# The end of the first batch: when w_out's last pieces are converted, batch 1's x is turned and half of the second products run

## The chip, the core and the metric

The kernel runs on one core of a Trainium2 chip. The core's engines run side by side, each through its own instructions in a fixed order, and wait for one another through semaphores: TensorE (PE, with its weight loads shown as PEld), VectorE (DVE), ScalarE (ACT), GpSimd (POOL, all but unused here), and SyncE (SP), which here only issues DMAs. The metric is the time of one execution on the device, in microseconds (us); smaller is better.

## The reference, cut to what matters

Eight batches of 512 tokens and 32 states, in 8 heads of 64, go through a cross attention in both directions. Its rows, 544 per batch and 512 wide, then go through two dense layers with an activation between them.

```python
# x: (8, 8, 512, 64)   state: (8, 8, 32, 64)   w_in: (512, 2048)   w_out: (2048, 512)
scores = scale * np.matmul(x, state.transpose(0, 1, 3, 2))
a = np.exp(scores - scores.max(-1, keepdims=True)); a /= a.sum(-1, keepdims=True) + 1e-09
xread = np.matmul(a, state)
scores2 = scale * np.matmul(state, x.transpose(0, 1, 3, 2))
a2 = np.exp(scores2 - scores2.max(-1, keepdims=True)); a2 /= a2.sum(-1, keepdims=True) + 1e-09
sread = np.matmul(a2, x)
x = np.concatenate([xread, sread], axis=2)      # then (B*544, 512)
h = x @ w_in
g = h * erf(np.maximum(h, 0.0) + np.log1p(np.exp(-np.abs(h))))    # h * erf(softplus(h))
out = g @ w_out
```

The two weight matrices arrive as 64-bit floats and are turned into 32-bit floats on the chip.

## The kernel before

**Weights.** `weight` fetches a piece of 1 MB into a buffer `raw` (three of them in turn) and converts it there: two ACT operations (L127, L128) and three DVE operations (L129, L130, L131). w_in and w_out come in eight pieces each, two pieces of each for one group of hidden features. There are four groups (`NG`) of four tiles of 128 features.

**The first batch.** Batch 0 is worked while the weights arrive, group by group, in the loop at L600. `mixed(0, g)` multiplies the states into w_in (L328: small products, 64 rows deep and 32 columns wide each, in two PSUM banks named `at`), and ACT and DVE copy one bank each to `m` (L330). `hidden` forms four banks `h` of first products (L420) in two PSUM buffers; from each, ACT writes a softplus (L427) and DVE a copy `hs` (L428), and both must be done before the buffer takes the next bank but one. `finish` takes erf on ACT (L432) and multiplies on DVE (L433). `project` is the second product (L438): 16 matmuls for a group, four for each of the banks `o` 0 to 3. It runs one group late: the second product of group 2 is issued behind the first product of group 3.

**The last group, g = 3.** Here other work is woven in. `rest` is the second half of batch 0's attention: turn the weights (L210 on PE, copies L212 on ACT), read the tokens (L224), scale (L229 on DVE), turn the result (L234). `states(1)` (L162) and `attention(1)` begin batch 1: x is turned on DVE (L284), PE forms the scores (L177, again 64 by 32 tiles), ACT copies them to `sc` (L181), and a chain on DVE and ACT makes the attention weights `aT` (L293 to L302). `prepare(1, ...)` makes `m` for two groups of batch 1 by four more calls of `mixed`, with `combine_m` adding them up on DVE (L339 to L342). `combine_a` does the same for `aT` (L352 to L355). `combine_w` (L460) makes sums of w_out's blocks, three of them into the `raw` buffers; all later second products use them.

In the kernel before, the two last pieces of w_out are fetched with the others, but their conversion is put off: `convert` (L625) holds the functions, and L637 issues them behind the copies of batch 1's scores (`marks[0]`).

**From batch 1 on** the first products (L375, `hidden7`) and the second products (L488, `project7`) use seven products where eight would stand, and the second product of the group before is interleaved with the first product of the group that runs. The first time, while batch 1's first group runs, the group that is interleaved is group 3 of batch 0 (L438, `pending` at L650), and its four banks are copied out at L447.

**What sets the order.** The program is written as a stream of calls, and a scheduler places each engine's instructions. `tc.issue_after(m)` (in `behind`) holds what stands within it until the instruction `m` in the scheduler's order. A group of instructions once placed runs in that order on its engine, whatever becomes ready first.

In the names, `o_336` to `o_339` are the four banks of batch 0's second products, and `o_1011` to `o_1014` those of batch 1's first half.

Of the kernel before, what the change touches and what calls it, by code (L numbers as in the profile page):

```python
# [8 lines left out]
F32 = mybir.dt.float32  # L9
U32 = mybir.dt.uint32  # L10
ALU = mybir.AluOpType
# [5 lines left out]
def kernel(  # L17
# [17 lines left out]
    nc = tc.nc  # L35
# [70 lines left out]

    fetched = []

    def weight(dst, src, shape, later):

        if src.dtype == F32:
            fetched.append(nc.sync.dma_start(out=dst, in_=src))
            return lambda: None
        i = shape[1]
        raw = act.tile([P, 2 * shape[0] * i], U32, name="raw", bufs=3)
        fetched.append(nc.sync.dma_start(out=raw.rearrange("p (o i) -> p o i", i=2 * i),
                                         in_=src.bitcast(U32)))  # L120
        words = raw.rearrange("p (n w) -> p n w", w=2)
        lo, hi = words[:, :, 0], words[:, :, 1]
        dst = dst.rearrange("p o i -> p (o i)")
        d = dst.bitcast(U32)

        def convert():
            nc.scalar.activation(out=dst, in_=hi.bitcast(F32), func=ACTF.Copy, scale=2.0 ** -112)  # L127
            nc.scalar.activation(out=lo, in_=lo, func=ACTF.Copy, scale=2.0 ** -29)  # L128
            nc.vector.tensor_scalar(d, d, 3, None, op0=ALU.logical_shift_left)  # L129
            nc.vector.tensor_tensor(d, d, lo, op=ALU.add)  # L130
            return nc.vector.scalar_tensor_tensor(out=d, in0=hi, scalar=0x80000000, in1=d,  # L131
                                                  op0=ALU.bitwise_and, op1=ALU.bitwise_or)
        return convert if later else convert()

    gw = GF * P

    def weights_in(j):
        return weight(w_in[:, j],
                      moe_w_in[:, 2 * P * j:2 * P * j + 2 * P].rearrange("(k p) f -> p k f", p=P),
                      (NK, 2 * P), False)  # L140

    def weights_out(j, later=False):
        return weight(w_out[:, 2 * j:2 * j + 2, :],
                      moe_w_out[2 * P * j:2 * P * j + 2 * P].rearrange("(t p) e -> p t e", p=P),
                      (2, d_model), later)

    spare = ps_o.tile([P, d_model], F32, name="o3")

# [21 lines left out]
    def scores(b, xT):  # L170


        s2 = [ps_at.tile([P, S], F32, name="at") for _ in range(2)]
        for i in range(NI):
            for e in range(2):
                r, q = slice(D * e, D * e + D), slice(Ns * i, Ns * i + Ns)
                on_pe = nc.tensor.matmul(out=s2[e][q, :], lhsT=stT[b][r, q], rhs=xT[r, i, :],  # L177
                                         start=True, stop=True)
        sc = att.tile([P, 2, S], F32, name="sc")
        for e in range(2):  # L180
            last = nc.scalar.copy(sc[:, e], s2[e])  # L181
        marks[:] = last, on_pe
        return sc, last
# [94 lines left out]
    def attention(b):  # L278

        xq = xq_t.pop(b)
        xT = att.tile([P, NI, S], F32, name="xT")
        nc.vector.transpose(out=xT.rearrange("p i t -> p (i t)"),  # L284
                            in_=xq.rearrange("p i m d -> p (i m d)"))
        if b + 1 < B:
            load_xq(b + 1)
        sc, _ = scores(b, xT)
        yield
        both = att.tile([P, NI, S], F32, name="xT")  # L290
        aT[b] = keep.tile([P, 2, S], F32, name="aT")
        for e in range(2):
            nc.vector.transpose(out=both[:, e], in_=sc[:, e])  # L293
            a = both[:, e].rearrange("p (k n) -> p k n", n=Ns)
            m1 = small.tile([P, NC * NI], F32, name="m1")
            nc.vector.reduce_max(out=m1, in_=a, axis=AX.X)
            nc.vector.tensor_tensor(a, a, over(m1), op=ALU.subtract)  # L297
            nc.scalar.activation(out=a, in_=a, func=ACTF.Exp, scale=scale)
        z2 = weigh_tokens(sc, both[:, 2:4])
        for e in range(2):  # L300
            normalise(both[:, e].rearrange("p (k n) -> p k n", n=Ns))
            nc.vector.transpose(out=aT[b][:, e], in_=both[:, e])  # L302
        yield
        a2T = turn_weights(both[:, 2:4])
        yield
        sn = read_tokens(b, a2T, z2)
        if b + 1 < B:
            load_x(b + 1)
        yield
        turn_read(b, sn)  # L310
        yield

    m_t = {}

    def mixed(b, g, parts=1):

        m_t[b, g] = mix.tile([P, 2, gw], F32, name="m")
        return [mixed_part(b, g, j, parts) for j in range(parts)]

    def mixed_part(b, g, j, parts):  # L320
        n = gw // parts
        mg = m_t[b, g][:, :, n * j:n * j + n]
        fs = slice(2 * g + j, 2 * g + j + 2 // parts)
        ps = [ps_at.tile([P, gw], F32, name="at")[:, 0:n] for _ in range(2)]
        for i in range(NI):
            for e in range(2):
                r, q = slice(D * e, D * e + D), slice(Ns * i, Ns * i + Ns)
                nc.tensor.matmul(out=ps[e][q, :], lhsT=stT[b][r, q],  # L328
                                 rhs=w_in[r, fs, i, :], start=True, stop=True)
        return nc.scalar.copy(mg[:, 0], ps[0]), nc.vector.tensor_copy(mg[:, 1], ps[1])  # L330

    def combine_m(b, g):

# [97 lines left out]
    def finish(s, hs):  # L431
        return (nc.scalar.activation(out=s, in_=s, func=ACTF.Erf),  # L432
                nc.vector.tensor_tensor(s, s, hs, op=ALU.mult))  # L433

    def project(gT, g, acc, rs=range(NC), ts=range(GF)):
        for r in rs:
            for i in ts:
                nc.tensor.matmul(out=acc[r], lhsT=gT[:, i, P * r:P * r + P],  # L438
                                 rhs=w_out[:, GF * g + i, :],
                                 start=(g == 0 and i == 0),  # L440
                                 stop=(g == NG - 1 and i == GF - 1))
                yield
# [90 lines left out]
    def begins(b):  # L533
        return 1 - b % 2
# [24 lines left out]
    def done(steps):  # L559
        for _ in steps:  # L560
            pass
# [4 lines left out]
                side[n]()  # L566
            yield

    def prepare(b, g):
        for j in range(2):  # L570
            mixed(b, 2 * g + j)
        combine_m(b, g)

    def begin(on_pe, on_act, on_dve):
# [5 lines left out]
    def behind(marks, f, *args):  # L580
        with ExitStack() as order:
            for m in marks:
                order.enter_context(tc.issue_after(m.ins))
            return f(*args)
# [15 lines left out]
    for g in range(1, NG):  # L600

        if g == 1:
            for j in range(2):
                made = behind(at, weights_in, 2 + j)
            done(project(gT, 0, acc, range(2)))
            at, = mixed(0, 1)
            behind([made], weights_out, 2)
            made = behind(at, weights_out, 3)
            done(project(gT, 0, acc, range(2, 3)))
        else:  # L610
            if g == 2:
                behind([made], weights_in, 4)
                behind(banks[1][:2], weights_in, 5)
                done(project(gT_, 0, acc, range(3, 4), range(GF - 1)))
            else:
                for j in range(2):
                    behind(banks[j][:2], weights_in, 2 * g + j)
            at, = mixed(0, g)
            if g == 2:
                done(project(gT_, 0, acc, range(3, 4), range(GF - 1, GF)))  # L620
            if g < NG - 1:
                for j in range(2):
                    behind(at, weights_out, 2 * g + j)
        if g == NG - 1:
            convert = [weights_out(2 * g + j, True) for j in range(2)]  # L625
            behind(fetched[-1:], load_st)
            behind(fetched[-1:], load_xq, 1)
            behind(done_, rest)
            load_x(1)
            states(1)  # L630
            turn = attention(1)
        gT_, (gT, hs, banks) = gT, hidden(0, range(GF * g, GF * g + GF), 0, S)
        at = done_ = finish(gT, hs)
        if g == NG - 1:

            behind([banks[1][1], at[0]], next, turn)
            for f in convert:  # L637
                behind(marks[:1], f)
            done(behind(marks[1:], project, gT_, g - 1, acc, range(1)))
            next(turn)  # L640
            prepare(1, begins(1))
            at = [combine_a(1)]
            done(behind(marks[1:], project, gT_, g - 1, acc, range(1, NC)))
        elif g > 1:
            done(project(gT_, g - 1, acc))
    prepare(1, 1 - begins(1))
    done(turn)
    last = behind(at, combine_w)

# [67 lines left out]
```

## Time and profile before

| | before |
|---|---|
| median of 3 runs | 783.2 us (782.07 to 783.7) |
| the profiled execution | 784.38 us, of which its span is 782.6 us |
| PE busy | 760.7 us, 97% of the span |
| DVE busy | 504.4 us, 64% |
| ACT busy | 383.6 us, 49% |
| chain of work that ended last | PE 79%, DVE 9%, ACT 4% |

A row of the timeline gives the start in us, the length in us, engine, line, operation, tiles (written and read), shape and count, and in brackets the idle time before it with what ended it. The length of a merged row reaches to the end of its last instruction, which overlaps the next row; the step from one row's start to the next is what it costs the engine. A 32-bit matmul leaves two records, so "x8" of L438 is four matmuls (a transpose by the identity, L210, leaves one). A row of the window view gives the stretch, its length, the busy time of PE, PEld, DVE, ACT and POOL with the number of records, the granted TensorE clock (1.00 is full speed), the DMA share and GB/s. In the view of waits a row reads: who waited, for whom, total us, how often, the longest.

### The profile page before, as it was taken

The numbers are of one execution on the slowest core, as the hardware profiler recorded it, in microseconds if no ns is written. First come the engines' busy times: TensorE is split into PE (matmuls) and PEld (weight loads), VectorE is DVE, ScalarE is ACT, GpSimd is POOL, SyncE is SP. The second block draws the span as 40 slices with busy tenths as digits, with TensorE's granted clock in tenths as the row PEclk, the third lists the DMA queues.
The fourth block names the chain that finished last, engine by engine and source line by source line (L and its number), as shares of the span: only waits on it lengthen the run. The fifth ranks groups of instructions, "written<-read, shape, count | busy, mean of one in ns | idle before, by whom it ended". The sixth has DMA issues, their size and how long they took to land.

```text
span 782.6 us, 11868 instructions
## 1 busy us (share of the span) xinstructions
PE 760.7 (97%) x4980; PEld 600.8 (77%) x4980; DVE 504.4 (64%) x757; ACT 383.6 (49%) x490; POOL 0.7 (0%) x6
## 2 busy tenths in 40 slices
PE   8998989989999999999999999999999999999997
PEld 7533431679888888888888888888889889998886
DVE  3888558786768666675767576947595665453431
ACT  5867543375446444554455444554464444443320
POOL 0000000000000000000000000000000000000000
PEclk9999995999999999999999999999999999999999
DMA  7675830332004200302012200320000000000001
GB/s 219 214 240 192 180 59 14 82 68 55 28 1 82 54 14 14 66 27 45 28 30 53 54 28 2 80 56 28 1 28 1 28 1 28 1 28 1 28 0 28
DMA packets 106557, 42.71 MB, mean 55 GB/s; under 512 B 96008, under 2 KB 96008, under 8 KB 106504
## 3 DMA queue, kind: packets, MB, share of 16 engines
q1 hardware_dynamic: 104392, 41.43, 19.9%
q8 instruction: 39, 0.64, 0.3%
q10 hardware_dynamic: 2112, 0.52, 0.3%
q14 instruction: 14, 0.11, 0.0%
HBM read 33.03 MB, written 8.91 MB: 54 GB/s over the span
## 4 chain that ended last, share of the span: by engine, by line
PE 79%; DVE 9%; ACT 4%; issue 1%; DVEq 0%; ACTq 0%
PE o L488 40%; PE h L375 20%; PE h L420 6%; PE o L438 6%; PE at L328 5%; ACT s L432 2%; DVE s L433 1%; DVE hs L382 1%; PE at L224 1%; ACT L432 1%; DVE ot L498 1%; PE at L210 1%; DVE m L197 1%; DVE z L187 1%; DVE xT L297 1%
## 5 line engine op out<-in xcount | busy, mean ns | idle before, releaser
L433 DVE TENSOR_TENSOR s<-s,hs 128x2048 f32<-128x2048 f32 x34 | 77.9, 2292 | 76.2 <-ACT s L432 76.1
L488 PE MATMUL o<-w_out,s 128*128 128x256 f32 x480 | 118.2, 381 | 0.0
L488 PE MATMUL o<-raw,hs 128*128 128x256 f32 x480 | 116.4, 385 | 0.0
L488 PE MATMUL o<-w_out,hs 128*128 128x256 f32 x480 | 115.4, 381 | 0.0
L488 PEld LDWEIGHTS o<-raw,hs 128*128 128x128 f32 x480 | 88.4, 190 | 31.3 <-issue 20.1
L381 ACT ACTIVATE s<-hs 128x512 f32<-128x512 f32 x112 | 70.6, 630 | 71.8 <-DVE hs L382 71.5
L488 PEld LDWEIGHTS o<-w_out,hs 128*128 128x128 f32 x480 | 90.0, 190 | 16.3 <-issue 4.2
L375 PEld LDWEIGHTS h<-aT,m 128*128 128x128 f32 x672 | 86.3, 195 | 11.6 <-issue 5.2
L488 PEld LDWEIGHTS o<-w_out,s 128*128 128x128 f32 x480 | 85.6, 192 | 8.4
L375 PE MATMUL h<-aT,m 128*128 128x128 f32 x672 | 88.1, 280 | 2.4 <-ACT s L385 2.4
L382 DVE TENSOR_TENSOR hs<-hs,h 128x512 f32<-128x512 f32 x84 | 57.5, 684 | 44.5 <-PE h L375 44.3
L438 PE MATMUL o<-w_out,s 128*128 128x512 f32 x128 | 63.6, 637 | 5.3 <-DVE w_out L131 4.4
L382 DVE TENSOR_TENSOR hs<-s,h 128x512 f32<-128x512 f32 x56 | 38.4, 686 | 46.8 <-PE h L375 46.4
L432 ACT ACTIVATE s<-s 128x2048 f32<-128x2048 f32 x34 | 65.0, 1911 | 0.4
L375 PE MATMUL h<-sy,sx 128*128 128x128 f32 x448 | 59.2, 275 | 0.0
L488 PE MATMUL o<-raw,s 128*128 128x256 f32 x240 | 57.7, 379 | 0.0
L375 PEld LDWEIGHTS h<-sy,sx 128*128 128x128 f32 x448 | 56.6, 192 | 1.5
L385 ACT COPY s<-h 128x512 f32<-128x512 f32 x28 | 16.3, 582 | 81.8 <-PE h L375 81.8
L438 PEld LDWEIGHTS o<-w_out,s 128*128 128x128 f32 x128 | 24.3, 200 | 37.8 <-issue 28.9
L390 ACT COPY hs<-h 128x512 f32<-128x512 f32 x28 | 16.3, 583 | 63.7 <-PE h L375 63.7
L488 PEld LDWEIGHTS o<-raw,s 128*128 128x128 f32 x240 | 43.6, 191 | 4.8
L328 PE MATMUL at<-w_in,stT 64*32 64x512 f32 (+1 forms) x528 | 43.8, 624 | 1.4 <-ACT sc L181 0.7
(100 smaller groups left out, 914.9 us busy)
## 6 DMA issues: line engine op xcount, KB each, us to landing
raw<-in_moe_w_in_dram SPq DMA_DIRECT2D x8, 1024.0 KB, 5.3
raw<-in_moe_w_out_dram SPq DMA_DIRECT2D x8, 1024.0 KB, 5.0
out_dram<-ot SPq DMA_DIRECT2D x32, 256.0 KB, 2.0
x<-in_x_dram SPq DMA_DIRECT2D x60, 128.0 KB, 2.9
xq<-in_x_dram SPq DMA_DIRECT2D x112, 64.0 KB, 2.1
x<-in_x_dram ACTq DMA_DIRECT2D x4, 128.0 KB, 3.9
out_dram<-ot SPq DMA_DIRECT2D x8, 64.0 KB, 1.7
st<-in_state_dram SPq DMA_DIRECT2D x8, 56.0 KB, 4.4
```

What stands on the lines that cost most here:

```text
L187: nc.vector.reduce_sum(out=z1, in_=a, axis=AX.X)
L328: nc.tensor.matmul(out=ps[e][q, :], lhsT=stT[b][r, q], rhs=w_in[r, fs, i, :], start=True, stop=True)
L375: last = nc.tensor.matmul(out=bank[:, q], lhsT=x[:, q], rhs=y, start=(first and i == 0), stop=(i == GF - 1), skip_group_check=not first)
L381: nc.scalar.activation(out=s[:, k], in_=hs[:, k], func=ACTF.Softplus)
L382: add = lambda o, x, y: nc.vector.tensor_tensor(o, x, y, op=ALU.add)
L385: nc.scalar.copy(m1, p)
L390: nc.scalar.copy(c11, p)
L420: on_pe = nc.tensor.matmul(out=hp[:, n * j:n * j + n], lhsT=lhsT, rhs=rhs, start=(k == 0), stop=(k == len(ops) - 1))
L432: return (nc.scalar.activation(out=s, in_=s, func=ACTF.Erf), nc.vector.tensor_tensor(s, s, hs, op=ALU.mult))
L433: nc.vector.tensor_tensor(s, s, hs, op=ALU.mult))
L438: nc.tensor.matmul(out=acc[r], lhsT=gT[:, i, P * r:P * r + P], rhs=w_out[:, GF * g + i, :], start=(g == 0 and i == 0), stop=(g == NG - 1 a ...
L488: nc.tensor.matmul(out=acc[bank][:, E2 * c:E2 * c + E2], lhsT=lhs[:, i, :], rhs=rhs[:, g, i, :], start=(first and i == 0 and c == 0), stop ...
```

## The change

Three things move, all around group 3 of batch 0; what is computed stays as it was.

- **w_out's two last pieces** are converted like the others, issued behind the copy `m` of `mixed(0, 3)`; `convert` and the argument `later` go.
- **batch 1's x is turned** (and its scores formed) behind the DVE copy of the last bank of group 3's first product, and `finish` of group 3 is held behind that turn. `finish` stood ahead of it.
- **half of group 2's second product** (banks 2 and 3) is issued behind the scores; before, that was three banks of four, with one bank ahead of the `prepare`. Now banks 0 and 1 are written ahead of it.
- The four `mixed` calls of the two `prepare` calls at this place have both their copies on ACT; before, one was on ACT and one on DVE.

```diff
@@ weight
-        def convert():
-            nc.scalar.activation(out=dst, in_=hi.bitcast(F32), func=ACTF.Copy, scale=2.0 ** -112)
...
-        return convert if later else convert()
+        nc.scalar.activation(out=dst, in_=hi.bitcast(F32), func=ACTF.Copy, scale=2.0 ** -112)
...
@@ attention
-        nc.vector.transpose(out=xT.rearrange("p i t -> p (i t)"),
+        turned = nc.vector.transpose(out=xT.rearrange("p i t -> p (i t)"),
...
         sc, _ = scores(b, xT)
+        marks.append(turned)
@@ mixed_part
-        return nc.scalar.copy(mg[:, 0], ps[0]), nc.vector.tensor_copy(mg[:, 1], ps[1])
+        return nc.scalar.copy(mg[:, 0], ps[0]), copy(mg[:, 1], ps[1])
@@ the loop over groups
-            if g < NG - 1:
-                for j in range(2):
-                    behind(at, weights_out, 2 * g + j)
+            for j in range(2):
+                behind(at, weights_out, 2 * g + j)
         if g == NG - 1:
-            convert = [weights_out(2 * g + j, True) for j in range(2)]
...
-        at = done_ = finish(gT, hs)
-        if g == NG - 1:
+        if g < NG - 1:
+            at = done_ = finish(gT, hs)
+        else:
 
-            behind([banks[1][1], at[0]], next, turn)
-            for f in convert:
-                behind(marks[:1], f)
-            done(behind(marks[1:], project, gT_, g - 1, acc, range(1)))
+            behind(banks[3][1:2], next, turn)
+            scored, turned = marks[1:]
+            behind([turned], finish, gT, hs)
+            done(project(gT_, g - 1, acc, range(2)))
             next(turn)
-            prepare(1, begins(1))
+            prepare(1, begins(1), nc.scalar.copy)
             at = [combine_a(1)]
-            done(behind(marks[1:], project, gT_, g - 1, acc, range(1, NC)))
-        elif g > 1:
+            behind([scored], lambda: done(project(gT_, g - 1, acc, range(2, NC))))
+        if g == 2:
             done(project(gT_, g - 1, acc))
-    prepare(1, 1 - begins(1))
+    prepare(1, 1 - begins(1), nc.scalar.copy)
```

Line numbers of the changed kernel are smaller by two or three: L438 is L436 there, L328 is L326, L177 is L174, L375 is L373, L488 is L486, L210 is L207, L127 and L128 are L125 and L126, L212 is L209, L427 is L425.

The first place is ACT, from the copy of `mixed(0, 3)` on. Before:

```order
L330 COPY m<-at 128x512
L212 COPY sc<-at 128x512 x2
L427 ACT_TABLE_LOAD
L427 ACTIVATE s<-h 128x512
L235 COPY sT<-at 128x4x32
L164 COPY stT<-at 128x128
L427 ACTIVATE s<-h 128x512 x3
L432 ACT_TABLE_LOAD
L432 ACTIVATE s<-s 128x2048
L181 COPY sc<-at 128x512 x2
L127 ACTIVATE w_out<-raw 128x1024
L128 ACTIVATE raw<-raw 128x1024
```

In the changed kernel, at the same place on ACT:

```order
L328 COPY m<-at 128x512
L125 ACTIVATE w_out<-raw 128x1024
L126 ACTIVATE raw<-raw 128x1024
L125 ACTIVATE w_out<-raw 128x1024
L126 ACTIVATE raw<-raw 128x1024
L209 COPY sc<-at 128x512 x2
L425 ACT_TABLE_LOAD
L425 ACTIVATE s<-h 128x512 x2
```

The conversions stand 10 rows earlier, ahead of the copies of the turned weights and of all four softplus of group 3's banks, instead of behind the copies of batch 1's scores. On DVE their six operations move likewise, from between the steps of batch 1's weights to ahead of the scaling L229.

The second place is PE around batch 1's scores (`at<-xT,stT`) and the `mixed` calls (`at<-w_in,stT`). Before, from the last first product of batch 0 on:

```order
L420 MATMUL h<-aT,m 128x512 x4
L438 MATMUL o_336<-w_out,s 128x512 x2
L438 MATMUL o_337<-w_out,s 128x512 x4
L438 MATMUL o_338<-w_out,s 128x512 x4
L438 MATMUL o_339<-w_out,s 128x512 x4
L177 MATMUL at<-xT,stT 32x512 x8
L328 MATMUL at<-w_in,stT 32x512 x8
L438 MATMUL o_336<-w_out,s 128x512
L328 MATMUL at<-w_in,stT 32x512 x4
```

In the changed kernel:

```order
L418 MATMUL h<-aT,m 128x512 x4
L436 MATMUL o_337<-w_out,s 128x512 x4
L174 MATMUL at<-xT,stT 32x512 x8
L436 MATMUL o_338<-w_out,s 128x512
L326 MATMUL at<-w_in,stT 32x512 x8
L436 MATMUL o_338<-w_out,s 128x512
L326 MATMUL at<-w_in,stT 32x512 x8
L436 MATMUL o_338<-w_out,s 128x512 x2
L436 MATMUL o_339<-w_out,s 128x512 x4
L326 MATMUL at<-w_in,stT 32x512 x8
L373 MATMUL h<-aT,m 128x128 x3
```

Before, 14 matmuls of group 2's second product stand ahead of the scores, and what is interleaved with the `mixed` calls belongs to group 3's second product, which reads w_out's last pieces. Now four stand there ahead of the scores (the two of bank 0 moved up among the first products), and eight of group 2's, which reads older pieces, stand behind them.

The third place is PE around the scores of batch 2, at the end of batch 1's first group. Before:

```order
L438 MATMUL o_339<-w_out,s 128x512
L375 MATMUL h<-aT,m 128x128 x4
L375 MATMUL h<-sy,sx 128x128 x4
L177 MATMUL at<-xT,stT 32x512 x8
L375 MATMUL h<-aT,m 128x128 x4
L488 MATMUL o_1011<-w_out,s 128x256 x4
```

In the changed kernel:

```order
L436 MATMUL o_338<-w_out,s 128x512 x3
L174 MATMUL at<-xT,stT 32x512 x8
L436 MATMUL o_338<-w_out,s 128x512
L436 MATMUL o_339<-w_out,s 128x512 x4
L373 MATMUL h<-aT,m 128x128 x4
L373 MATMUL h<-sy,sx 128x128 x4
L486 MATMUL o_1011<-w_out,s 128x256 x4
```

The last five matmuls of group 3's second product now stand behind these scores; before, all were ahead of them, and the next row needed what ACT does after the scores. From some 20 rows further on, PE's order is the same in both kernels to the end.

On SP, the loads of batch 2's x (L72) now stand ahead of the first store of batch 0's output instead of behind it.

More of the change, by code (lines that the diff above doesn't have):

```diff
@@ L107, with weight @@
     fetched = []
-    def weight(dst, src, shape, later):
+    def weight(dst, src, shape):
         if src.dtype == F32:
             fetched.append(nc.sync.dma_start(out=dst, in_=src))
-            return lambda: None
+            return
         i = shape[1]
@@ L124, in weight @@
         d = dst.bitcast(U32)
-        def convert():
[L127 to L132, printed above, removed]
-        return convert if later else convert()
+        nc.scalar.activation(out=dst, in_=hi.bitcast(F32), func=ACTF.Copy, scale=2.0 ** -112)
+        nc.scalar.activation(out=lo, in_=lo, func=ACTF.Copy, scale=2.0 ** -29)
+        nc.vector.tensor_scalar(d, d, 3, None, op0=ALU.logical_shift_left)
+        nc.vector.tensor_tensor(d, d, lo, op=ALU.add)
+        return nc.vector.scalar_tensor_tensor(out=d, in0=hi, scalar=0x80000000, in1=d,
+                                              op0=ALU.bitwise_and, op1=ALU.bitwise_or)
     gw = GF * P
@@ L139, in weights_in, with weights_out @@
                       moe_w_in[:, 2 * P * j:2 * P * j + 2 * P].rearrange("(k p) f -> p k f", p=P),
-                      (NK, 2 * P), False)
-    def weights_out(j, later=False):
+                      (NK, 2 * P))
+    def weights_out(j):
         return weight(w_out[:, 2 * j:2 * j + 2, :],
                       moe_w_out[2 * P * j:2 * P * j + 2 * P].rearrange("(t p) e -> p t e", p=P),
-                      (2, d_model), later)
+                      (2, d_model))
     spare = ps_o.tile([P, d_model], F32, name="o3")
@@ L283, in attention @@
         xT = att.tile([P, NI, S], F32, name="xT")
-        nc.vector.transpose(out=xT.rearrange("p i t -> p (i t)"),
-                            in_=xq.rearrange("p i m d -> p (i m d)"))
+        turned = nc.vector.transpose(out=xT.rearrange("p i t -> p (i t)"),
+                                     in_=xq.rearrange("p i m d -> p (i m d)"))
         if b + 1 < B:
@@ L313, with mixed, mixed_part @@
     m_t = {}
-    def mixed(b, g, parts=1):
+    def mixed(b, g, parts=1, copy=nc.vector.tensor_copy):
         m_t[b, g] = mix.tile([P, 2, gw], F32, name="m")
-        return [mixed_part(b, g, j, parts) for j in range(parts)]
-    def mixed_part(b, g, j, parts):
+        return [mixed_part(b, g, j, parts, copy) for j in range(parts)]
+    def mixed_part(b, g, j, parts, copy):
         n = gw // parts
@@ L567, in accompanied, with prepare @@
             yield
-    def prepare(b, g):
+    def prepare(b, g, copy):
         for j in range(2):
-            mixed(b, 2 * g + j)
+            mixed(b, 2 * g + j, copy=copy)
         combine_m(b, g)
```

## Prediction

> **What bounds the kernel now.** The first page says what kind of loss to look for.
>
> ```profile
> PE 760.7 (97%) x4980; PEld 600.8 (77%) x4980; DVE 504.4 (64%) x757; ACT 383.6 (49%) x490; POOL 0.7 (0%) x6
> PEclk9999995999999999999999999999999999999999
> ```
>
> PE is busy for 97% of the span, so little seems left. But the seventh of the 40 slices (117 to 137 us) was granted half the clock: a busy PE is slow there. That is where the change works. Next, the view of PE's waits; these five lie in the stretch that changes.
>
> ```profile
> PE o L438 <- DVE w_out L131: 4.4, 1, 4.4
> PE h L375 <- ACT s L385: 2.4, 1, 2.4
> PE at L328 <- ACT sc L181: 0.7, 1, 0.7
> PE at L177 <- DVE xT L284: 0.4, 1, 0.4
> PE at L224 <- ACT sc L212: 0.3, 1, 0.3
> ```
>
> The largest wait is for the conversion of w_out's last pieces. Third, the view by stretches, cut where the clock changed:
>
> ```profile
> 62.18:65.59 3.41, 1.38 (x4) 0.59 (x4) 1.63 (x2) 3.41 (x4) 0.00 (x0) 1.00 0.75 273
> 65.59:69.01 3.42, 3.42 (x6) 1.36 (x5) 3.30 (x5) 3.40 (x4) 0.00 (x0) 0.50 0.00 0
> 109.97:113.38 3.41, 2.68 (x20) 0.51 (x19) 0.42 (x1) 1.04 (x3) 0.00 (x0) 1.00 0.67 110
> 113.38:116.79 3.41, 1.17 (x16) 0.18 (x14) 3.41 (x6) 3.41 (x5) 0.00 (x0) 1.00 0.74 123
> 116.79:140.69 23.90, 21.73 (x62) 5.47 (x66) 16.65 (x34) 8.21 (x14) 0.00 (x0) 0.50 0.06 16
> 161.17:164.58 3.41, 1.09 (x16) 0.21 (x16) 1.30 (x1) 3.40 (x5) 0.00 (x0) 1.00 0.64 133
> 164.58:167.99 3.41, 3.24 (x12) 2.97 (x13) 3.41 (x6) 1.23 (x3) 0.00 (x0) 0.50 0.72 118
> ```
>
> All cuts lie on one grid of 3.41 us. A window in which PE was busy for 1.1 to 1.4 us is followed by half the clock; one with 2.68 is not. After 65.59 and 164.58 one window of dense full-size matmuls brings the clock back. After 116.79 seven windows pass, though PE is nearly all busy: there it alternates between full-size matmuls (L438) and the small ones of `mixed` (L328). So the stall of 4.4 us costs far more than itself. Last, PE's timeline for the prices:
>
> ```profile
> 87.02 1.09 PE L328 MATMUL at<-w_in,stT 64*32 64x512 f32 x16
> 88.03 1.12 PE L438 MATMUL o<-w_out,s 128*128 128x512 f32 x2
> 89.00 1.04 PE L210 MATMUL at<-ident,xT 128*128 128x128 f32 x8
> 89.87 1.02 PE L420 MATMUL h<-aT,m 128*128 128x512 f32 x2
> 90.83 1.10 PE L224 MATMUL at<-x,sc 128*32 128x64 f32 x64
> ...
> 99.05 12.18 PE L438 MATMUL o<-w_out,s 128*128 128x512 f32 x28
> ...
> 112.98 1.58 PE L328 MATMUL at<-w_in,stT 64*32 64x512 f32 x16 [0.73 <-ACT sc L181]
> 118.95 2.07 PE L438 MATMUL o<-w_out,s 128*128 128x512 f32 x2 [4.40 <-DVE w_out L131]
> 120.96 1.93 PE L328 MATMUL at<-w_in,stT 64*32 64x512 f32 x8
> 122.82 2.07 PE L438 MATMUL o<-w_out,s 128*128 128x512 f32 x2
> ...
> 140.29 1.23 PE L328 MATMUL at<-w_in,stT 64*32 64x512 f32 x8
> 141.45 0.49 PE L375 MATMUL h<-aT,m 128*128 128x128 f32 x2
> ...
> 158.86 1.05 PE L375 MATMUL h<-aT,m 128*128 128x128 f32 x8
> 159.75 1.06 PE L375 MATMUL h<-sy,sx 128*128 128x128 f32 x8
> ...
> 164.75 2.08 PE L375 MATMUL h<-aT,m 128*128 128x128 f32 x8 [2.40 <-ACT s L385]
> ...
> 169.03 1.05 PE L375 MATMUL h<-aT,m 128*128 128x128 f32 x8
> ...
> 187.26 1.89 PE L488 MATMUL o<-w_out,s 128*128 128x256 f32 x8
> ```
>
> At full clock, one `mixed` (16 records) costs 1.01 (87.02 to 88.03), one matmul of L438 or L420 0.86 (12.1 over 14), four of L375 0.89 (158.86 to 159.75). At half clock half a `mixed` costs 1.86 (120.96 to 122.82) where 0.51 is due: the small matmuls suffer most.
>
> **The ledger.** PE does the same matmuls in both kernels between 89.00, where batch 0's weights are turned, and 187.26, where the second matmul set of L488's second group begins; behind that point its order is the same. Of these 98.26 us the kernel before loses:
> - the five waits, 0.73 + 4.40 + 0.45 + 2.40 + 0.29 = 8.27 (the timeline's digits, or the view's);
> - 1.58 - 1.01 = 0.57 inside the first `mixed` at 112.98, which waits for its second bank;
> - half clock from 118.95 to 140.29: 21.34 for five matmuls of L438 (4.30), five halves of `mixed` (2.53) and four of L375 (0.89), so 13.62; and 1.16 - 0.51 = 0.65 in the next half;
> - half clock from 164.75 to 169.03: 4.28 for four of L375 (0.89) and four of L488, half as wide as L438 (1.73), so 1.66.
>
> That is 24.77 lost and 73.49 of work at full clock. The time after is this work plus the waits that the new order makes.
>
> **Part by part.** I follow the new order with rows of before; ACT and DVE:
>
> ```profile
> 88.19 0.58 ACT L330 COPY m<-at 128x512 f32<-128x512 f32 x1 [0.71 <-PE at L328]
> 113.30 1.20 ACT L127 ACTIVATE w_out<-raw 128x1024 f32<-128x1024 f32 x1
> 116.45 1.17 ACT L128 ACTIVATE raw<-raw 128x1024 uint32<-128x1024 uint32 x1
> 105.31 2.30 DVE L284 STREAM_TRANSPOSE xT<-xq 128x2048 f32<-128x2048 f32 x1
> 112.96 1.31 DVE L293 STREAM_TRANSPOSE xT<-sc 128x512 f32<-128x512 f32 x2 [5.34 <-ACT sc L181]
> 132.33 0.42 DVE L355 TENSOR_TENSOR sy<-aT,sy 128x256 f32<-128x256 f32 x1
> 142.21 2.28 DVE L460 TENSOR_TENSOR raw<-w_out 128x2048 f32<-128x2048 f32 x1
> ```
>
> *Conversions.* The 4.40 goes, and with it the cause of the long half clock. ACT takes them at 88.8; four operations are 4.3 (113.30 to 117.6), so to 93.1. Behind them on ACT wait the copies of the turned weights, then the softplus of all four banks. PE covers this with the transposes (0.87) and four matmuls of L420 (3.44), to 93.3; reading the tokens can start at the first copy, 93.1 + 0.6: **0.35 lost**. DVE finishes its six operations at about 96.3 and scales the read tokens at 96.7; PE, after reading (1.07) and two of L438, is there at 96.4: **0.4 lost**. The first banks' softplus and copies end near 97.9, when PE comes to the third bank: nothing lost, with no margin.
>
> *The turn behind the last bank.* PE's last bank ends at about 101.4; softplus 0.6, the bank's copy 0.7 and the turn 2.3 bring x to 105.1. PE covers with four of L438 (3.44), to 104.8: **0.4 lost**. Nothing is lost to `finish` behind it: what reads its product (group 3's second product) now starts some 14 us later.
>
> *Both copies on ACT, seconds behind the scores.* Where `mixed` follows on banks that ACT still empties, PE waits for the second of two copies. This happens three times: 0.3, 0.3 and 0.5, **1.1 lost**. It replaces 0.73 and 0.57. DVE loses four copies of 0.6.
>
> *DVE's chain.* From the turn of the scores (112.96) to the end of L355 (132.75) DVE took 19.8 without a pause; without the six conversion operations (5.7) and two copies (1.2) within it, 12.8. Behind `finish` it starts at 107.5 and ends at 120.3; PE needs its sum of L353 (two short operations earlier, 119.8) at 119.1: from the scores at 105.2 it has these (1.0), eight of L438 (6.9), four `mixed` with their waits (4.0 + 1.1) and four quarter matmuls (0.9). **0.7 lost**. Then come three sums of L460 (2.2 each), four sums of `combine_m` (0.6 each) and the scaling, to 129.9; PE, with three of L375's sets of four (2.6), four of L438 (3.4), the transposes (0.9) and the reading (1.1), is there at 127.8 and waits for that scaling: **2.2 lost**. Here DVE is the bound.
>
> *Scores of batch 2.* Five matmuls of L438 (4.3) now stand behind them while ACT finishes erf and its copies, so the waits of 0.45 and 2.40 and the window at half clock go. Behind them batch 1's second group needs a sum of L382 from DVE, which there stands behind some 5 us of batch 2's weights, two operations of 0.6 more than PE's own work covers: of this, **0.7 lost**.
>
> The new waits are 5.85. PE reaches the second point at 89.00 + 73.49 + 5.85 = 168.3 instead of 187.3: **18.9 less**. Nothing later pays it back: SP's reordered loads and stores (first stores of an output that ends 600 us later) are covered, and the steady part is the same. The profiled execution, 784.4, becomes 765.5; the median of the runs is 1.2 below that execution, so **764.3**. The terms not seen in before's trace are bounded so: the new waits are at least 0 (all covered: 758.4) and, if each is half as large again, 8.8 (767.2). I take the worked-out value, since DVE's 12.8 is taken from the very same operations.
>
> The Trainium skill speaks for a full clock in the new order: "TensorE: Matmul & The Clock Gate", section "Why this matters for your kernels", asks for no PE-idle gap over about 3 us, and by it the new gap of 2.2 is free. The row at 62.18 differs: a window 1.38 us busy, all of it full-size matmuls, was followed by half the clock. By the page the sum stays as it is; by the row one window at half clock may be added.
>
> **The rivals.**
> 1. *The clock falls again.* The gap of 2.2 leaves a window that holds it 1.24 us busy, like 62.18; between 105 and 110 only two full-size matmuls stand among small ones and waits, though PE is busy as long as in the window at 109.97. For: where the grid falls against the kernel is open. Against: dense runs follow each place (six of L438; L375 and L438 from 130 on). One window at half clock costs 1.7, three 5.1; what falls before 127 is partly covered by PE's waits for DVE. 766.0 to 769.4.
> 2. *DVE's chain is longer than worked out*, as by waits for ACT's exponentials that now stand behind `mixed`'s copies. A tenth of its 22.4 us from 107.5 to 129.9 is 2.2: 766.5.
> 3. *The clock is held down.* Mechanism: the alternation of `mixed` and L438, which held it seven windows at 116.79, stands from 105 to 119 again. Before, this cost 14.3 over 23.9 us. To end slower than before, half clock must last until the 18.9 and the covered 2.9 are used up, over 40 us at half speed, twelve windows from 105 on; then 783 and more, some 786. Against: the 5.2 us of pure L438 at 110, whereas 3.3 us of L375 and L438 ended it before.
> 4. *The pieces aren't there.* If the stall came from the fetch and not from the order, nothing is gained: 783. Against: before, ACT's conversions follow its scores' copies in the order without a pause, and the view names the conversion, no DMA.
>
> **How the numbers follow.** The forecast, 762 to 766, 0.62; the first rival 0.20, the second 0.08, the third and fourth 0.03 each; 0.04 for less than 762, if the new waits are mostly covered. The range leaves out the third and fourth and the ends: 760.5 (two thirds of the new waits covered) to 769.4 (three windows). A difference of 0.2%, 1.6 us, is about what a measurement of this kernel can tell. Only the third and fourth rivals fall outside faster: faster 0.94, same 0.03, slower 0.03.
>
> **What would show it.** Right: no wait of L436 for w_out; ACT's conversions at about 89 to 93; the clock at 1.00 from 105 to 168; the scores (L174) at about 105; PE waiting about 2 us for the scaling L226 near 128; no wait for the copy of L383; the second group of L486 near 168. Wrong: a slice of PEclk under 9 between 105 and 150 (rivals 1 and 3), a wait for DVE near 119 or 128 over 4 us (rival 2), or new waits for ACT at the third bank near 98.

## The result, and the profile after

The changed kernel takes 764.4 us in the median of 4 runs (763.58 to 764.78), the kernel before 783.45 in these runs (782.07 to 783.81): a ratio of 0.9759, with a 95% interval of 0.9742 to 0.9776. The forecast was 764.3.

The changed kernel's page, in the lines that answer to those of before:

```profile
PE 746.6 (98%) x4980; PEld 597.0 (78%) x4980; DVE 501.7 (66%) x753; ACT 384.3 (50%) x493; POOL 0.7 (0%) x6
PEclk9999999999999999999999999999999999999999
```

The slice at half clock is gone, and PE is busy for 14.1 us less (746.6 against 760.7) with the same 4980 matmul records: it did the same work, for the most part at a higher clock; the experiments below find a second reason, how the small products are issued. The view of PE's waits, for the stretch that changed, and the view by stretches across it:

```profile
PE at L231 <- DVE sn L226: 1.9, 2, 1.6
PE h L373 <- DVE hs L380: 1.3, 6, 0.4
PE at L174 <- DVE xT L281: 0.3, 1, 0.3
```

```profile
105.00:150.00 45.00, 43.01 (x310) 23.14 (x311) 41.64 (x63) 26.84 (x46) 0.00 (x0) 1.00 0.45 94
```

The waits of 4.4 for w_out, of 2.4 for ACT's copy and of 0.7 and 0.4 are gone (the 0.4 stood at batch 2's scores; the 0.3 listed here stands at batch 1's); the largest that is new is PE's wait for the scaling of the read tokens, 1.6. The clock (third number from the end) is 1.00 over the whole stretch. PE's timeline of the changed kernel, at the ledger's two points and at the places that the forecast named:

```profile
88.38 1.04 PE L207 MATMUL at<-ident,xT 128*128 128x128 f32 x8
89.25 3.60 PE L418 MATMUL h<-aT,m 128*128 128x512 f32 x8
92.90 1.15 PE L221 MATMUL at<-x,sc 128*32 128x64 f32 x64
...
104.97 1.09 PE L174 MATMUL at<-xT,stT 64*32 64x512 f32 x16 [0.29 <-DVE xT L281]
...
117.81 1.51 PE L326 MATMUL at<-w_in,stT 64*32 64x512 f32 x16
...
126.40 1.88 PE L436 MATMUL o<-w_out,s 128*128 128x512 f32 x4
129.91 0.33 PE L231 MATMUL at<-ident,sn 128*128 128x128 f32 x1 [1.63 <-DVE sn L226]
...
167.25 1.89 PE L486 MATMUL o<-w_out,s 128*128 128x256 f32 x8
```

From the first point to the second PE took 98.26 us before and 78.87 (88.38 to 167.25) now: 19.4 less. From the second point to the end of the span both took 595.3 (782.6 - 187.26 and 762.6 - 167.25), so nothing was paid back later. The first point itself came 0.6 us earlier, for a reason outside the change (last section).

### The profile page after: what moved, and what is told of

It is laid out like the page before. It is cut to its first block, busy times and chain, and to the rows that moved or that the text cites. A ratio compares the mean times of both kernels' runs of the same rounds, so it can differ in the third digit from the quotient of the medians.

```text
span 762.6 us, 11865 instructions
## 1 busy us (share of the span) xinstructions
PE 746.6 (98%) x4980; PEld 597.0 (78%) x4980; DVE 501.7 (66%) x753; ACT 384.3 (50%) x493; POOL 0.7 (0%) x6
## 4 chain that ended last, share of the span: by engine, by line
PE 76%; DVE 11%; ACT 4%; issue 2%; DMA 1%; SPq 0%; DVEq 0%
PE o L486 42%; PE h L373 20%; PE h L418 6%; PE at L326 3%; PE o L436 2%; ACT s L430 2%; DVE s L431 1%; DVE hs L380 1%; ACT L430 1%; DVE m L194 1%; PE at L221 1%; DVE z L184 1%; DVE xT L295 1%; DVE ot L496 1%; DMA raw<-in_moe_w_in_dram 1%
## 5 line engine op out<-in xcount | busy, mean ns | idle before, releaser
L486 PE MATMUL o<-w_out,s 128*128 128x256 f32 x480 | 117.7, 380 | 0.0
L486 PE MATMUL o<-raw,hs 128*128 128x256 f32 x480 | 116.3, 385 | 0.0
L486 PE MATMUL o<-w_out,hs 128*128 128x256 f32 x480 | 115.4, 381 | 0.0
L486 PEld LDWEIGHTS o<-raw,hs 128*128 128x128 f32 x480 | 88.4, 190 | 31.4 <-issue 20.1
L486 PEld LDWEIGHTS o<-w_out,hs 128*128 128x128 f32 x480 | 89.8, 190 | 16.3 <-issue 4.2
L486 PEld LDWEIGHTS o<-w_out,s 128*128 128x128 f32 x480 | 84.9, 191 | 8.1
L373 PEld LDWEIGHTS h<-aT,m 128*128 128x128 f32 x672 | 84.4, 192 | 6.4 <-issue 1.6
L373 PE MATMUL h<-aT,m 128*128 128x128 f32 x672 | 85.6, 276 | 0.4 <-DVE hs L380 0.4
L436 PE MATMUL o<-w_out,s 128*128 128x512 f32 x128 | 59.1, 600 | 0.9 <-DVE s L431 0.9
L373 PE MATMUL h<-sy,sx 128*128 128x128 f32 x448 | 59.5, 275 | 0.0
L373 PEld LDWEIGHTS h<-sy,sx 128*128 128x128 f32 x448 | 56.7, 192 | 2.2 <-ACT hs L388 0.6
L486 PE MATMUL o<-raw,s 128*128 128x256 f32 x240 | 57.9, 379 | 0.0
L486 PEld LDWEIGHTS o<-raw,s 128*128 128x128 f32 x240 | 43.5, 190 | 4.7
L436 PEld LDWEIGHTS o<-w_out,s 128*128 128x128 f32 x128 | 23.1, 190 | 30.0 <-issue 28.8
```

Of the source, the lines that this page charges most:

```text
L373: last = nc.tensor.matmul(out=bank[:, q], lhsT=x[:, q], rhs=y, start=(first and i == 0), stop=(i == GF - 1), skip_group_check=not first)
L486: nc.tensor.matmul(out=acc[bank][:, E2 * c:E2 * c + E2], lhsT=lhs[:, i, :], rhs=rhs[:, g, i, :], start=(first and i == 0 and c == 0), stop ...
```

## The experiments

Ten runs were made to find what the 19 us hang on: one that fills the stall so that the half clock goes, seven with one part undone or some parts alone, the changed kernel once more, and one that goes on from the changed kernel. The chip is not the same for all, so times are compared with the kernel before on the same chip, and with the changed kernel where it ran there.

**The half clock alone.** Twenty matmuls of the identity fill PE's stall in the kernel before; their result is not used.

```diff
             next(turn)
-            prepare(1, begins(1))
+            first_m = mixed(1, 2 * begins(1))
+            idle = ps_h.tile([P, S], F32, name="h")
+            with tc.issue_after(on_mixed[-1].ins):
+                for _ in range(20):
+                    nc.tensor.matmul(out=idle[:, 0:P], lhsT=ident, rhs=ident,
+                                     start=True, stop=True)
+            mixed(1, 2 * begins(1) + 1)
+            combine_m(1, begins(1))
```

> The kernel before, with 20 matmuls of the identity by itself (128x128, about 0.22 us each, into an unused first-product bank) put on PE behind the first mixed call, where PE stood idle for 4.4 us; their result is read by nobody. Nothing is converted earlier. Theory (the ledger: most of the loss is the half clock that the stall sets off): the granted clock stays at 1.00 through 117 to 141 us, the 14.3 us of half clock shrink to what the waits for DVE and ACT then show (about 4), and the time is about 772. Rival (half the clock is a by-product, and the stretch is bound by the waits of the small products for their banks): the time stays at 783 to 784.

It took 771.45 against 783.35 for the kernel before on the same chip (ratio 0.9846, 0.9822 to 0.987): 11.9 us gained by useless work. Its view by stretches and its timeline:

```profile
105.00:150.00 45.00, 43.83 (x313) 24.21 (x311) 39.10 (x57) 20.98 (x34) 0.00 (x0) 1.00 0.31 71
```

```profile
113.90 4.73 PE L647 MATMUL h<-ident 128*128 128x128 f32 x40
118.47 1.03 PE L440 MATMUL o<-w_out,s 128*128 128x512 f32 x2
119.57 1.06 PE L329 MATMUL at<-w_in,stT 64*32 64x512 f32 x8
120.56 1.12 PE L440 MATMUL o<-w_out,s 128*128 128x512 f32 x2
...
128.32 1.09 PE L329 MATMUL at<-w_in,stT 64*32 64x512 f32 x16
129.34 1.16 PE L377 MATMUL h<-aT,m 128*128 128x128 f32 x8
```

The stall is as long as it was (L440 starts at 118.47, before at 118.95), but the clock stays up, although small and full-size matmuls alternate behind it again. So half clock was the larger part of the loss. The order is not quite that of before: the three `mixed` calls behind the stall run as four halves and a whole one, where six halves stood, and the waits at batch 2's scores are smaller. The rows show one thing more: half a `mixed` (x8) costs 0.99 (119.57 to 120.56) at full clock, where the forecast had taken 0.51, half of a whole one. A whole one (x16) costs 1.02. So eight of these 64 by 32 products run in the time of four. And a single matmul of L440 between small products costs 1.06 (120.56 to 121.62), where 0.86 is the price in a dense run.

**The first part alone**: w_out's last pieces converted early in the kernel before.

```diff
-            if g < NG - 1:
-                for j in range(2):
-                    behind(at, weights_out, 2 * g + j)
+            for j in range(2):
+                behind(at, weights_out, 2 * g + j)
...
-            for f in convert:
-                behind(marks[:1], f)
```

> The kernel before with the first part of the change alone: w_out's last pieces are converted behind the copy of mixed(0, 3); the turn of x, finish, the second products' order and the copies on DVE stay. First theory (the stall of 4.4 us and the half clock behind it are the loss, whatever else stands there): the wait for w_out goes, the clock stays up, about 767. Second theory (the order of PE's fillers matters as much: with the last pieces ready early, PE runs 26 second products ahead of batch 1's scores, and nothing is left to cover batch 1's first products and the scores of batch 2): waits for DVE of 1 to 3 us each at L375 and before L488, 778 at full clock, up to 783 if the clock falls at these waits.

779.16 (ratio 0.9945, 0.9927 to 0.9964): a gain of 4.2 only. Its timeline shows why:

```profile
99.80 20.76 PE L438 MATMUL o<-w_out,s 128*128 128x512 f32 x48
120.49 1.09 PE L177 MATMUL at<-xT,stT 64*32 64x512 f32 x16
...
142.99 0.45 PE L234 MATMUL at<-ident,sn 128*128 128x128 f32 x1 [2.50 <-DVE sn L229]
143.23 0.42 PE L162 MATMUL at<-ident,st 128*128 128x128 f32 x1
145.70 2.08 PE L375 MATMUL h<-aT,m 128*128 128x128 f32 x8 [2.04 <-DVE hs L382]
148.56 2.07 PE L375 MATMUL h<-sy,m 128*128 128x128 f32 x8 [0.78 <-DVE hs L382]
```

With the weights ready, the wait for w_out is gone, but PE runs 24 second products in a row ahead of the scores, and has none left when batch 1's first products wait for DVE. The waits move from 114 to 140 us, and the clock falls there: it is 0.58 from 140 to 155 us, and the four matmuls at 145.70 span 2.08 where 1.05 is usual. The second theory is the right one.

**The first part undone**: the changed kernel with the conversion put off as before.

```diff
             behind([turned], finish, gT, hs)
+            for f in convert:
+                behind(marks[:1], f)
```

> The changed kernel with the first part undone: the conversion of w_out's last pieces is put off behind ACT's copies of batch 1's scores, as before; the turn behind the last bank, the half of the second products behind the scores and the copies on ACT stay. First theory (the place of the conversion makes the gain): the wait for w_out or a stall of about 4 us at the mixed calls comes back, and with it the half clock; 775 to 784. Second theory (the second products of group 2 behind the scores cover the conversion wherever it stands): waits of 0.5 to 1.2 us at the mixed calls, none for w_out, the clock at full speed; 764, within 1 us of the changed kernel.

763.44 (0.9752, 0.9732 to 0.9772), no slower than the changed kernel. No wait for w_out is among PE's waits, and from 105 to 150 us the clock is 1.00:

```profile
105.00:150.00 45.00, 44.14 (x301) 24.18 (x302) 42.08 (x61) 28.04 (x43) 0.00 (x0) 1.00 0.38 79
```

With the other parts there, the early conversion adds nothing.

**The second part undone**: `finish` ahead of the turn.

```diff
-            behind(banks[3][1:2], next, turn)
-            scored, turned = marks[1:]
-            behind([turned], finish, gT, hs)
+            at = finish(gT, hs)
+            behind(at[1:], next, turn)
+            scored, turned = marks[1:]
```

> The changed kernel with the second part undone: finish of group 3 (erf, product) stands ahead of the turn of batch 1's x again. Theory: batch 1's chain on DVE starts later by the wait for erf and the product, about 4.7 us, PE covers that by moving second products ahead of the scores, and they are missing later: 770, at most one window of half clock (1.7) more. Rival (finish ahead of the turn costs nothing, since PE has other work): 764 to 765.

771.94 (0.9859, 0.9832 to 0.9887), 7.5 over the changed kernel's 764.4, and 8.5 over the kernel with the first part undone, which ran on the same chip. PE's waits name the product of `finish`, now needed at once by second products that PE has moved ahead of the scores, and again at batch 1's first second products:

```profile
PE o L436 <- DVE s L431: 3.7, 2, 2.8
PE o L486 <- DVE s L431: 2.8, 1, 2.8
```

Half clock follows both waits of 2.8 in this profile, from 107.3 to 110.7 and from 151.7 to 158.5 us, which is more than the one window that was expected; the profiled run is also the slowest of the four (774.43).

**The third part undone**: group 2's second products without an order behind the scores, beside the changed kernel once more.

```diff
-            done(project(gT_, g - 1, acc, range(2)))
+            done(project(gT_, g - 1, acc))
...
-            behind([scored], lambda: done(project(gT_, g - 1, acc, range(2, NC))))
```

> The changed kernel with the third part undone: all four banks of group 2's second product are written without an order behind the scores, so 14 matmuls less 2 run ahead of what they were to cover. Theory (fillers that run early are missing later): the scores wait on PE behind 12 second products, start 7 us later, DVE's chain with them, and PE then waits 1.7, 0.7 and 2.9 us for DVE: 767, up to 769 with one window of half clock. Rival (the order behind the scores does nothing once the conversion is early): 764 to 765.

> The changed kernel once more, on the chip of the three that follow, to compare with: 764 to 765.

767.71 (0.9796, 0.9776 to 0.9815) against 764.53 (0.9743, 0.9722 to 0.9764) on the same chip: 3.2 more, as expected. PE waits 2.8 for the product of `finish` before L486 and 1.0 for a sum of `combine_a`, and half clock follows the 2.8 from 148.3 to 151.7 us.

**The fourth edit undone**: one copy of each `mixed` on DVE again.

```diff
-            prepare(1, begins(1), nc.scalar.copy)
+            prepare(1, begins(1), nc.vector.tensor_copy)
```

> The changed kernel with the fourth edit undone: the mixed calls' second copies are on DVE again. Theory: four copies of 0.6 us go back into DVE's chain, and PE waits for two of them at the mixed calls (1.6 and 0.8 us), but not at the scaling; the sum is even: 764 to 765. Rival (DVE is the bound from 107 to 130 us, so each of its operations shows): 2.4 more, 767.

763.42 (0.9741, 0.9722 to 0.976): the same. In its timeline the wait for the scaling is gone from this place, and halves of `mixed` are back:

```profile
109.17 1.06 PE L326 MATMUL at<-w_in,stT 64*32 64x512 f32 x8
110.16 1.98 PE L436 MATMUL o<-w_out,s 128*128 128x512 f32 x4
112.74 1.06 PE L326 MATMUL at<-w_in,stT 64*32 64x512 f32 x8 [0.59 <-DVE m L195]
...
128.34 1.88 PE L436 MATMUL o<-w_out,s 128*128 128x512 f32 x4
130.06 0.27 PE L231 MATMUL at<-ident,sn 128*128 128x128 f32 x1
```

Two banks emptied by two engines come free at different times, PE issues the four products of each as they do, and pays 0.99 twice.

**The third part alone, and the second and third together**, in the kernel before, conversion late and copies on both engines.

```diff
-            done(behind(marks[1:], project, gT_, g - 1, acc, range(1)))
+            scored, = marks[1:]
+            done(project(gT_, g - 1, acc, range(2)))
...
-            done(behind(marks[1:], project, gT_, g - 1, acc, range(1, NC)))
+            behind([scored], lambda: done(project(gT_, g - 1, acc, range(2, NC))))
```

> The kernel before with the third part alone: banks 2 and 3 of group 2's second product are ordered behind batch 1's scores, banks 0 and 1 are written ahead of the prepare; conversion, finish and the DVE copies stay as before. Theory (second products that need no new weights, put behind the scores, are enough to cover the late conversion and to keep the clock up; what the turn adds is the earlier start of batch 1's chain): no wait for w_out, clock 1.00 from 105 to 150, batch 1's scores at about 107; 770 to 773. Rival (the conversion has to move too): a wait for w_out of some us, half clock, 778 or more.

> The second and third parts together, without the earlier conversion and with one of the mixed calls' copies on DVE as before. Theory (the parts add: the turn gives the third part alone another 3.4 us, the time by which the scores come sooner): 766 to 769, the rest to 764 being mixed calls that run in halves because their two banks come free from two engines at different times. Rival (the earlier conversion or the copies are needed for the gain): 772 or more.

The third part alone: 771.12 (0.9833, 0.9809 to 0.9857), 12.6 of the gain. With the second: 764.57 (0.9763, 0.9744 to 0.9781), all of it by the medians and better than expected. In its profile the stretch up to the first point, which the edits don't touch, is short (the point lies at 86.70 us, in the changed kernel at 88.38), and from there to the end of the span it takes 675.9, the changed kernel 674.2; so the rest that the theory gave to the halves of `mixed`, some 2 us, may well be there. The third part alone leaves a wait for the turn, and the full clock that was expected does not come: two windows at half clock stand behind the wait (0.50 from 107 to 113 us):

```profile
102.73 1.02 PE L438 MATMUL o<-w_out,s 128*128 128x512 f32 x2
107.15 1.96 PE L177 MATMUL at<-xT,stT 64*32 64x512 f32 x16 [3.40 <-DVE xT L284]
109.04 2.07 PE L438 MATMUL o<-w_out,s 128*128 128x512 f32 x2
111.04 1.96 PE L328 MATMUL at<-w_in,stT 64*32 64x512 f32 x16
112.93 5.45 PE L438 MATMUL o<-w_out,s 128*128 128x512 f32 x12
```

At half clock the scores, one matmul of L438 and a whole `mixed` take 1.89, 2.00 and 1.89, and the dense run that follows is at full clock again (5.4 for six). That is 5.78 where 3.1 is due, so of the 6.6 by which the second part shortens this kernel, 3.4 are the wait and 2.7 the half clock behind it. One of the four runs took 768.07, with a mean clock of 1.000 where the other three have 0.992 to 0.995: that would fit a run without this half clock, but it has no trace.

**A step beyond the change**: w_out's three sums held behind the scaling for which PE waits.

```diff
-            nc.vector.tensor_scalar(sn[:, e], sr[:, e], z2[:, e:e + 1], None, op0=ALU.mult)
+            scaled[:] = nc.vector.tensor_scalar(sn[:, e], sr[:, e], z2[:, e:e + 1], None,
+                                                op0=ALU.mult),
...
-    last = behind(at, combine_w)
+    last = behind(scaled, combine_w)
```

> The changed kernel with w_out's three sums (combine_w) held on DVE behind the scaling of batch 1's read tokens; nothing else moves by hand. Theory (the wait of 1.6 us at the transpose of the read tokens is due to these sums, which nothing needs before the second products of batch 1): that wait goes and no other comes, 1.5 to 2.2 less than the changed kernel, 762 to 763. Rival (DVE's later sums then hold up the first products' additions or the second products): no gain, 764 or more.

761.59 (0.9718, 0.9696 to 0.974), in the median 2.9 below the changed kernel on the same chip, though the two intervals overlap. The profiles agree with a gain, of 2.3: from the first point to the end of the span it takes 671.9 (759.1 - 87.15), the changed kernel 674.2 (762.6 - 88.38). The other 1.2 by which the spans differ lie ahead of what the edit moves. On DVE:

```profile
122.48 0.47 DVE L228 TENSOR_SCALAR sn<-at,z 128x64 f32<-128x64 f32 x2
122.88 2.28 DVE L461 TENSOR_TENSOR raw<-w_out 128x2048 f32<-128x2048 f32 x1
125.07 0.68 DVE L383 TENSOR_TENSOR hs<-s,h 128x512 f32<-128x512 f32 x1
```

The scaling ends at 123 instead of 129.9, PE's largest wait there is 0.3, and the sums now stand between the first products' additions without holding them up.

## Why the prediction was right, point by point

- **The ledger's work and the second point.** PE was forecast at 168.3 from a start at 89.00, 79.3 us; it took 78.9. The new waits were forecast at 5.85 and are 5.4 by this (78.87 - 73.49).
- **The conversion's cost**, 0.35 and 0.4: reading the tokens starts 0.2 late (92.90, where the step of 3.45 from 89.25 ends at 92.70), and PE waits 0.3 for the scaling by its view (0.5 by the steps). The third bank waited for nothing.
- **The turn**, 0.4: 0.29. The scores start at 104.97, forecast 105.1.
- **The copies**, 1.1: by the steps 0.4 at each of the first two calls and 0.4 at the fourth. Of the 0.4 at the first two, 0.2 is the wait within the call (1.24 for 1.02) and 0.2 no wait: the matmul of L436 ahead of it costs 1.05 between small products.
- **DVE's chain**, 0.7 and 2.2: 0.3 and 1.8 (126.40 and 1.72 to 129.91). DVE is the bound there, as said; holding the sums back showed it.
- **Scores of batch 2**: no wait for ACT's copy, and 0.5 of the 0.7 for DVE's sum.
- **The first rival** (the clock falls at the gap of 2.2) did not come about: with the gap at 1.8 the clock stayed at 1.00 in both profiles of the changed kernel. That a gap of this size is always free isn't shown, and the reading that the prediction sets against this rival, by which gaps of up to about 3 us are free, does not hold here: half clock followed the wait of 2.40 before L375 in the kernel before, and one of 2.8 before L486 with the third part undone.
- **The mis-sized term** is "five halves of `mixed` (2.53)" with 0.65 for a sixth, and the sentence that the small matmuls suffer most from half clock. At full clock a half costs 0.99 and a single full-size matmul between small products 1.06, so half clock from 118.95 to 140.29 took some 10.0 (21.34 - 5.30 - 4.95 - 1.09, with the steps of the kernel with the dummy matmuls) and not 13.6, and 0.2 in the sixth half. Of the other 4.1, 2.9 is the price of issuing three `mixed` calls as six halves, and 1.2 is what the full-size matmuls cost more between small products. The sum stays, because the halves went with the half clock: both copies on ACT bring the calls together again. The dummy matmuls' 11.9 is about these 10.2 and the 1.7 of the window at 164.75, which went with them; what else changed in their order about cancels.
- **The wrong attribution** is in the step on the conversions: "The 4.40 goes, and with it the cause of the long half clock", put down to converting early. Converting early does take that wait away, but alone it gained 4.2, since other waits with half clock behind them came in its place; and with the other parts there, leaving it out cost nothing. The third part alone takes the wait away too, and gained 12.6: eight second products that need no new weights stand where PE had only products that need them. With the second part, either of the two goes far: 767.7 with the early conversion and the copies on ACT (the third part undone), 764.6 with the third. So what a part is worth depends on which others are there. The second part is worth 6.6 to 7.5 beside the third, and the forecast had booked it only as a wait of 0.4; what it does alone was not run. The ledger was blind to this: it summed the final order and never asked what each edit would do alone.
- **Luck in the last digit.** The profiled execution fell by 20.0 (784.4 to 764.4), 19.4 in the stretch and 0.6 ahead of it, where 18.9 was forecast; and the forecast took 1.2 off for the median, which now lies at the profiled execution. That the median came within 0.1 of the forecast is these two misses cancelling. The stretch itself was forecast within 0.5.

## What to carry to other kernels

A stall on a TensorE that is otherwise 97% busy is priced by what follows it: look at the granted clock behind each wait, and at how long it stays down. Filler work is a stock: work that could run any time belongs behind the point where the engine would starve, and making it ready earlier only spends it earlier. A ledger of one engine's work between two points that both kernels share gives a good total, but it doesn't say which edit earned it; for that the parts must be undone one by one.

## What the runs showed of the hardware

Four 64 by 32 products of 512 columns cost about as much as eight: 0.99 and 1.02 us at full clock, 1.86 and 1.89 at half. Eight of them fill the array's 128 by 128, and a batch of four leaves half of it empty.

The clock's 3.41 us grid falls differently against each execution: by steps of 3.41 from 65.59, the kernel before has an edge at 106.55 and the next at 109.97, while the half clock begins at 106.2 with the third part alone and at 107.3 with the second part undone. The same wait of 2.0 near 62 us, in code that the change doesn't touch, was followed by a window at half clock in the kernel before (65.59, in the prediction's rows) and in a second profile of the changed kernel, and not in its first. First profile, then second:

```profile
59.00:73.00 14.00, 11.77 (x41) 4.52 (x40) 12.00 (x13) 12.28 (x13) 0.00 (x0) 1.00 0.44 147
```

```profile
59.00:73.00 14.00, 11.77 (x37) 4.44 (x36) 12.03 (x13) 12.82 (x13) 0.00 (x0) 0.88 0.44 143
```

The changed kernel's second series of runs falls into two groups that would fit one such window, 762.86 and 762.89 (mean clock 0.999) against 764.53 to 764.94 (0.996 and 0.997); that each of these runs differs by it is argued, not shown. It is not the only difference ahead of the change: the first point lay between 86.70 and 89.00 us in the twelve profiles. In a series of one kernel, a difference of some 2 us may be this and not the edit.

Why the clock stayed low for seven windows in the kernel before, with PE busy in nearly all of that time, is open. One dense window ended it elsewhere, and with the clock up the alternation of small and full-size matmuls did not bring it down; that this alternation holds it down once it has fallen is the prediction's reading, and no run was made for it. Small products as such were no bar: with the third part alone the window from 109.6 to 113.0, in which PE was busy throughout, held a full-size matmul of L438 and a whole `mixed`, and full clock followed it. In the kernel before the `mixed` calls ran there as halves.
